# A fused retention and two-layer MLP kernel: three second-layer products of the last chunk's units by a second level of Strassen, with their sums on GpSimd

## The chip, the cores and the metric

The kernel runs on one core of a Trainium2 chip. Its time is device microseconds of one launch; the median of three runs before the change is 630.89 us (630.62 to 631.08). Five engines work from queues of their own, each in order: TensorE (PE, matrix products into PSUM), VectorE (DVE), ScalarE (ACT), GpSimd (POOL) and SyncE (SP, which starts transfers). Everything is computed in f32.

## The reference

A retention layer gives 3072 tokens of 512 features; a two-layer MLP with a leaky ReLU follows. Nearly all arithmetic lies in the MLP.

```python
state = np.zeros((B, H, D, D), dtype=np.float32)
for t in range(S):                                   # B, H, S, D = 4, 8, 768, 64
    state = gamma * state + np.einsum('bhd,bhe->bhde', k[:, :, t], v[:, :, t])
    y[:, :, t] = scale * np.einsum('bhd,bhde->bhe', q[:, :, t], state)
x = y.transpose(0, 2, 1, 3).reshape(B * S, H * D)    # 3072 x 512
h = x @ w_in                                         # 512 x 2048
out = np.maximum(0.01 * h, h) @ w_out                # 2048 x 512
```

## The kernel before

**Tiling.** The sequence is cut into six chunks c = 0 to 5 of 128 steps; with four batches a chunk is 512 tokens, held as 2 x 2 blocks of 256 x 256 (`x`, 128 partitions x 4 blocks x 2 x 256). The 2048 hidden features are four units u = 0 to 3 of 512. A unit of the first layer makes the hidden tile `g` (four blocks), a unit of the second adds g's product with 512 rows of w_out to the chunk's output tile `o` (the result is `os[c]`, four blocks).

**Strassen.** All these 2 x 2 block products are done with seven products M1 to M7 in place of eight, in the form that shares sums (Winograd's). A weight unit holds seven operands (blocks 0 to 3 and three sums); a moving tile holds four blocks and three differences, made by `differences` (L636, four DVE subtractions). Chunks 0 and 1 use one level: seven products of 256 x 256, each of four TensorE products with 256 columns. From chunk 2 on the loop at the end of the kernel goes over n = 0 to 15, with c = 2 + n // 4 and u = n % 4 (`at_of`), and uses two levels:

- The first layer is 7 x 7 = 49 products of 128 x 128, in two groups: `inner(n, 0)` has four of the outer seven (28 products), `inner(n, 1)` three (21). Its steps (L1390) run in the order M1, M5, M4, M6, M2, M3, M7; five results of a step are copied from PSUM by ACT (L1394 to L1402), the others are added by DVE. `outer(n, 0)` and `outer(n, 1)` (L1416) are two and five DVE additions that put the outer level together, and four `leaky` activations of ACT (L1432) follow on outer(n, 1).
- The second layer, for n = 3 to 14, is split. Four of the seven outer products are the *leaves* (`leaf_steps`, L1304): 28 products of 128 x 128 (L1311), in the step order M1, M5, M2, M6, M4, M3, M7. Their moving sums are made by POOL in `leaf_sums` (L1283, four instructions of 128 x 512 over the last blocks of the g tile), their results are kept apart and added to `os[c]` one unit later by `add_results` (L1333, one DVE addition 2048 wide). The other three outer products, operands 0, 4 and 5, are the *trunk* (`trunk`, L1344): 12 products of 256 columns (L1351), which pile up in the PSUM banks 5, 7 and 4 over the units of a chunk. `trunk_taken` (L1356) and its `rest` take them out once, after the chunk's last unit on this path: for chunk 5 in n = 14.
- n = 15, the last unit, has a plain one-level second layer (`output`, whose products are L674), in the order M1, M5, M6, M4, M2, M7, M3, with a store after each block of `os[5]` is complete; M3 goes in three pieces, each with a store of its own.

**Order.** The order is written out by hand; each engine takes its instructions as the loop issues them. In a pass n: add_results (the leaves of n - 1), differences of g(n), inner(n + 1, 0), outer(n + 1, 0), leaf_sums(n), trunk(n), inner(n + 1, 1), outer(n + 1, 1), the leaves of n with the leaky activations of n + 1 set between their copies. In n = 14 the leaky activations stand one by one between the first leaf steps, and differences of g(15) after the fourth.

**Banks.** PSUM has eight banks. inner uses 0 to 3, the leaves 0, 2, 1 and 6, the trunk 5, 7 and 4. In Strassen's steps M1's result is copied to the bank of M6 and M7, M2 is added on M1's bank, M3 on M5's and M7 on M6's, so each later product waits for the copy of the earlier.

The last passes of the loop before the change:

```python
        if leaves:
            moving = leaf_sums(n, behind if not scores_next else None)
            trunk(n, part)
...
        if last_leaves:
            rest = trunk_taken(n, os[c])
            if n + 2 == N2:
                rest()
```

Of the kernel before, what the change touches and what calls it, by code (L numbers as in the profile page):

```python
# [9 lines left out]
FP32 = mybir.dt.float32  # L10
# [6 lines left out]
ALU = mybir.AluOpType  # L17

C = 128
# [3 lines left out]
def kernel(  # L23
# [14 lines left out]
    nc = tc.nc  # L38
    NC = S // C
    DM = H * D  # L40
    HP = H // 2
    NU = DF // 512
    N = B * C // 2
# [4 lines left out]
    work = ctx.enter_context(tc.tile_pool(name="work", bufs=1))  # L48
# [31 lines left out]
    def unit(k):  # L80
        if k not in units:
            units[k] = unit_tile(k, f"w{k}")
        return units[k]
# [11 lines left out]
    step = dec[:, HP * C + NC * H :]  # L95
# [10 lines left out]
    AHEAD = 2  # L106
# [98 lines left out]
    def new_t(c, name):  # L205
        return work.tile([128, 3, 2, N], FP32, tag=f"t{c % 2}", name=name)

    def new_o(c, name="o"):
        return work.tile([128, 4, 2, N], FP32, tag=f"o{int(c > 0)}", name=f"{name}_{c}")
# [408 lines left out]
    def plus(out, a, b):  # L618
        return nc.vector.tensor_tensor(out=out, in0=a, in1=b, op=ALU.add)  # L619
# [186 lines left out]
    def tile_x(c):  # L806
        return work.tile([128, 4, 2, N], FP32, tag="x", bufs=2, name=f"x_{c}")
# [3 lines left out]
        return [x, new_t(c, f"t_{c}")]  # L811

    slot = [0]
    last_four = {}

    class Reversed:

# [6 lines left out]
    def new_g(c, u):  # L824
        i = slot[0]
        slot[0] = 1 - i
        both = work.tile([128, 7, 2, N], FP32, tag=f"g{i}", name=f"g_{c}_{u}")
        last_four[c, u] = both[:, 1:5]
        return u, both[:, 0:4], Reversed(both)

    def run(steps, at):
# [27 lines left out]
    x, t = xs[0]  # L859
# [25 lines left out]
    for s in range(2):  # L885
        part = mask[ts(s, 64), 0 : 3 - s : 2 - s]
# [3 lines left out]
    os = {}  # L890
# [18 lines left out]
    def scratch(name, n):  # L909
# [22 lines left out]
        out=dec[:, 0:n_gq], in_=spread.rearrange("p i n -> p (i n)")))  # L932
# [88 lines left out]
    made = {}  # L1021
# [48 lines left out]
    N2 = (NC - 2) * NU  # L1070

    def at_of(n):
        return 2 + n // NU, n % NU
# [78 lines left out]
    for u in range(NU):  # L1152
        for c in range(2) if u > 0 else ():
# [3 lines left out]
            at = rounds(1, 3)  # L1157
            at = put(at, **hidden_more.get((c, u), {}))
            run(hidden(c, u, *xs[c], *parts[c][1:]), at)
        for c in range(2 if u < NU - 1 else 1):  # L1160
            if u == 0:
                os[c] = new_o(c)
            at = rounds(1, 4 - c) if u < NU - 1 else {}
            at = put(at, **output_more.get((c, u), {}))
# [4 lines left out]
    bank = [ffs.tile([128, 4 * C], FP32, tag="ff", bufs=4, name=f"bank{i}") for i in range(4)]  # L1169
# [25 lines left out]
    def flat_of(part):  # L1195
        return part.rearrange("p i k n -> p (i k n)")
# [106 lines left out]

    def leaf_steps(n, moving):  # L1304

        ps = [bank[i].rearrange("p (i n) -> p i n", i=4) for i in (0, 2, 1, 6)]
        results = leaf_results(n)
        leaf_weights[:] = of_unit.pop(n, leaf_weights)
        for m, q, j, s in LEAVES:
            for i, to in enumerate(TARGETS):  # L1310
                nc.tensor.matmul(ps[q][:, to], lhsT=leaf_weights[i][j], rhs=moving[s][:, i],  # L1311
                                 start=(i == 0 and m in ("M1", "M5", "M4")), stop=True,
                                 skip_group_check=True)
            if m == "M1":
                nc.scalar.copy(out=ps[3], in_=ps[0])
            elif m == "M3":
                plus(results[:, :, 1], results[:, :, 1], ps[1])
            elif m == "M7":
                plus(results[:, :, 3], results[:, :, 3], ps[3])
            else:  # L1320
                nc.scalar.copy(out=results[:, :, {"M5": 3, "M4": 2, "M6": 1, "M2": 0}[m]],
                               in_=ps[q])
            yield

        plus(results[:, :, 2], results[:, :, 2], ps[3])
        plus(results[:, 2], results[:, 2], results[:, 3])
        if at_of(n)[1] > 0:
            unadded.append(lambda: plus(flat_of(os[at_of(n)[0]]), flat_of(os[at_of(n)[0]]),
                                        results.rearrange("p i q n -> p (i q n)")))

    unadded = []

    def add_results():  # L1333

        while unadded:
            unadded.pop()()
# [7 lines left out]
    def trunk(n, part):  # L1344

        u, g, gd = part
        first = n == FIRST_LEAVES or u == 0
        for x, sa, rhs in (("A", 0, g[:, 0]), ("C", 4, gd[:, 0]), ("B", 5, gd[:, 1])):
            for i in range(2):
                for k in range(2):  # L1350
                    nc.tensor.matmul(room[x][:, i, :],  # L1351
                                     lhsT=block(2 * u + 1, sa)[:, k, ts(i, 128)],
                                     rhs=rhs[:, k, :], start=(first and i == 0 and k == 0),
                                     stop=(k == 1), skip_group_check=True)
# [92 lines left out]
    def products(steps, n):  # L1447

        for _ in range(n):
            next(steps, None)  # L1450
# [38 lines left out]
    for n in range(N2):  # L1489
        c, u = at_of(n)  # L1490
        more, visiting, leaves = n + 1 < N2, visits(n), by_leaves(n)
        scores_next = visiting and following(c + 1, 2 * u)
        last_leaves = leaves and (u == NU - 1 or n + 2 == N2)
        if u == 0 and not leaves:
            os[c] = new_o(c)
        if u > 0:
            add_results()
        if more:
            differences(*gs[n][1:])
            if n > 0:  # L1500
                begun = inner_steps(n + 1, 0, held=visiting)
                products(begun, 1)
            while held:
                held.pop()()
            products(begun, 7)
        part = gs.pop(n)
        behind = None
        if visiting:
            if u == 0:
                xs[c + 1] = new_x(c + 1)  # L1510
            joint_visit(c + 1, 2 * u)
            if leaves:
                load_rows(n, range(4)[2 if u == 0 else 0 :])
        elif leaves and u == NU - 1:
            behind = sums_of_x(c + 1, 1)
        if more:
            outer(n + 1, 0)
        if leaves and u == 0:
            finish_chunk(c - 1)
            os[c] = new_o(c)  # L1520
        if visiting and u == 1:
            behind = differences(*xs[c + 1])
        elif c + 1 < NC and u == 2:
            behind = sums_of_x(c + 1, 0)
        if leaves:
            moving = leaf_sums(n, behind if not scores_next else None)
            trunk(n, part)
            if visiting and not scores_next:
                fill(6, 2, start=False)
        else:  # L1530
            steps = output(c, os[c], [part], u == 0, u == NU - 1, room=room if more else last_room,
                           order=FUSED if more else LAST, held=held if more else None)
            products(steps, 3)
        if last_leaves:
            rest = trunk_taken(n, os[c])
            if n + 2 == N2:
                rest()
        if scores_next and leaves:
            scores_of_pair(*scores_next, [bank[i] for i in (1, 6, 2, 3)], second_mask_last=True)
        elif scores_next:  # L1540
            scores_of_pair(*scores_next)
        if visiting:
            load_unit(n + 2, 0)
        if not leaves:
            products(steps, 1)
        if n in (0, 1):
            keep.append(sums_of_rows(n))
        if n in (1, 2):
            keep.append(sums_of_rows(n + 1, nc.gpsimd))
        if more:  # L1550
            inner(n + 1, 1)
            if last_leaves and n + 2 < N2:
                rest()
            for i in range(2) if visiting else ():
                ahead(c + 2, 2 * u + i)
            if keep:
                keep.pop(0)()
            if not leaves:
                products(steps, 1)
            later = [] if leaves else None  # L1560
            outer(n + 1, 1, later)
        if leaves:
            leaf = leaf_steps(n, moving)
            last_one = n + 2 == N2
            for count, ready in ((1, 1), (1, 1), (2, 2)) if last_one else (
                    (4, 2 if u == NU - 1 else 3), (1, 2 if u == NU - 1 else 1)):
                products(leaf, count)
                for _ in range(ready):
                    later.pop(0)()
            if last_one:  # L1570
                differences(*gs[n + 1][1:])
            products(leaf, 8)
            if last_one:
                add_results()
        else:
            products(steps, 3)
        if by_leaves(n + 1) and n + 1 >= NU:
            if not visits(n + 1):
                load_rows(n + 1)
            elif u == NU - 1:  # L1580
                load_rows(n + 1, range(2))
# [92 lines left out]
```

## Time and profile before

| what | value |
|---|---|
| median of three runs | 630.89 us |
| the profiled execution | 631.22 us |
| its span, first to last instruction | 629.3 us |
| TensorE clock granted | full speed throughout |
| n = 12: 546.43 to 568.84 us, DVE busy / ACT / POOL | 17.67 / 10.36 / 5.89 us of 22.41 |
| n = 13: 568.84 to 591.25 us | 15.34 / 10.20 / 5.49 us of 22.41 |
| n = 14: 591.25 to 613.65 us | 21.20 / 11.01 / 5.83 us of 22.40 |
| n = 15 and the last stores: 613.65 to 629.30 us | 10.77 / 0.70 / 0.00 us of 15.65 |

Times in the profile are microseconds from the span's start. A row of a timeline gives the start, the length, the engine, the line, the operation, the tiles written and read, the shape, how many instructions the row merges, and in brackets the idle time before it and what ended that. The busy time of TensorE overlaps from product to product, so the pace is read from the distance between starts. DVE's additions are all on L619 and its subtractions on L622, the lines of the helpers `plus` and `minus`: they are told apart by their tiles. DVE instructions without a dependence start some 0.08 us before the one ahead ends.

### The profile page before, as it was taken

Reading aid. Unit: us, or ns where it says so; the run is one execution under the profiler, and the core shown is the slowest. Engines: PE = TensorE matmul, PEld = TensorE weight load, DVE = VectorE, ACT = ScalarE, POOL = GpSimd, SP = SyncE. Lnnn points to the kernel's source line nnn. Section 1 sums busy time; section 2 is a strip of 40 time slices with the busy share of each in tenths; the row PEclk is TensorE's granted clock in tenths of the full one; section 3 lists DMA queues with packets and bytes.
Section 4 is the critical chain, followed back from the end, with each engine's and each line's share of the span. In section 5 each row is a group of like instructions: output and inputs, shape, how many; then the busy total and the mean of one; then the engine's idle time right before and its main releaser. Section 6 shows DMA issues by size and latency. Waiting matters only on the chain.

```text
span 629.3 us, 15220 instructions
## 1 busy us (share of the span) xinstructions
PE 622.8 (99%) x6375; PEld 572.2 (91%) x6375; DVE 512.4 (81%) x793; ACT 281.4 (45%) x543; POOL 105.8 (17%) x109
## 2 busy tenths in 40 slices
PE   8999999999999999999999999999999999999997
PEld 5888888888888889899999999999999999999996
DVE  5679769889979986679888968789968689977796
ACT  5876646446444114352433433534514435534540
POOL 2000000000010110105133052331250321333030
PEclk9999999999999999999999999999999999999999
DMA  8941425547782998396976996988478568678601
GB/s 328 405 143 34 126 75 193 167 133 252 243 296 73 347 333 272 101 339 190 349 228 215 283 333 240 324 280 280 150 257 298 156 216 281 209 264 278 205 1 68
DMA packets 105939, 140.99 MB, mean 224 GB/s; under 512 B 4488, under 2 KB 84232, under 8 KB 105872
## 3 DMA queue, kind: packets, MB, share of 16 engines
q1 hardware_dynamic: 105568, 139.41, 66.6%
q8 instruction: 50, 0.82, 0.5%
q10 hardware_dynamic: 304, 0.62, 0.3%
q14 instruction: 17, 0.14, 0.1%
HBM read 113.54 MB, written 26.48 MB: 222 GB/s over the span
## 4 chain that ended last, share of the span: by engine, by line
PE 94%; DVE 2%; ACT 1%; DMA 1%; issue 0%; SPq 0%; DVEq 0%; ACTq 0%
PE bank L1390 27%; PE bank L1311 12%; PE bank L1351 10%; PE bank L674 9%; PE C_h L674 4%; PE B_o L674 4%; PE A_h L674 4%; PE A_o L674 4%; PE C_o L674 4%; PE B_h L674 4%; PE D_o L674 2%; PE D_h L674 2%; PE d L695 2%; DMA raw<-in_weights_dram 1%; PE bank L371 1%; PE bank L453 1%
## 5 line engine op out<-in xcount | busy, mean ns | idle before, releaser
L619 DVE TENSOR_TENSOR made<-made,bank 128x512 f32<-128x512 f32 (+1 forms) x96 | 55.9, 617 | 39.8 <-PE bank L1390 35.9
L1390 PEld LDWEIGHTS bank<-x,wb 128*128 128x128 f32 x672 | 77.4, 192 | 1.2 <-ACT bank L1394 0.2
L1390 PE MATMUL bank<-x,wb 128*128 128x128 f32 x672 | 78.4, 276 | 0.0
L622 DVE TENSOR_TENSOR g<-g 128x512 f32<-128x512 f32 x96 | 64.0, 688 | 5.2 <-ACT g L1432 0.5
L1390 PE MATMUL bank<-x,wa 128*128 128x128 f32 x512 | 67.7, 275 | 0.0
L1394 ACT COPY bank<-bank 128x512 f32<-128x512 f32 (+1 forms) x32 | 16.6, 517 | 104.6 <-PE bank L1390 97.4
L1390 PEld LDWEIGHTS bank<-x,wa 128*128 128x128 f32 x512 | 62.7, 192 | 0.5 <-ACT made L1400 0.2
L1390 PE MATMUL bank<-t,wa 128*128 128x128 f32 x384 | 53.4, 275 | 0.0
L619 DVE TENSOR_TENSOR g<-made 128x512 f32<-128x512 f32 x64 | 49.0, 786 | 2.9
L1351 PE MATMUL bank<-g,w 128*128 128x256 f32 x216 | 48.5, 381 | 0.0
L1390 PEld LDWEIGHTS bank<-t,wa 128*128 128x128 f32 x384 | 48.0, 192 | 0.0
L1311 PE MATMUL bank<-g,w 128*128 128x128 f32 x368 | 47.0, 276 | 0.0
L1351 PEld LDWEIGHTS bank<-g,w 128*128 128x128 f32 x216 | 40.3, 190 | 5.4
L1311 PEld LDWEIGHTS bank<-g,w 128*128 128x128 f32 x368 | 43.8, 192 | 0.0
L1432 ACT ACTIVATE g<-g 128x512 f32<-128x512 f32 x64 | 37.7, 633 | 6.9 <-DVE g L619 6.9
L1290 POOL TENSOR_TENSOR x<-g 128x512 f32<-128x512 f32 x12 | 16.6, 1382 | 138.2 <-DVE t L622 40.1
L674 PE MATMUL bank<-g,w 128*128 128x256 f32 x168 | 38.0, 382 | 0.0
L674 PEld LDWEIGHTS bank<-g,w 128*128 128x128 f32 x168 | 31.3, 190 | 4.2
L619 DVE TENSOR_TENSOR o<-o,bank 128x512 f32<-128x512 f32 (+2 forms) x44 | 26.5, 633 | 9.8 <-ACT bank L788 4.2
L619 DVE TENSOR_TENSOR o<-o,w 128x2048 f32<-128x2048 f32 (+2 forms) x17 | 28.9, 1722 | 0.2
L674 PE MATMUL A_h<-x,w 128*128 128x256 f32 x112 | 26.6, 380 | 0.0
L163 POOL TENSOR_TENSOR in<-in,dec 128x512 f32<-128x512 f32 x2 | 2.4, 1232 | 139.7 <-DMA in<-in_kv_dram 139.7
(257 smaller groups left out, 1261.1 us busy)
## 6 DMA issues: line engine op xcount, KB each, us to landing
wa<-kept SPq DMA_DIRECT2D x16, 1344.0 KB, 8.7
w<-leaf_kept SPq DMA_DIRECT2D x44, 448.0 KB, 5.4
raw<-in_weights_dram SPq DMA_DIRECT2D x31, 512.0 KB, 4.4
wb<-kept SPq DMA_DIRECT2D x16, 896.0 KB, 6.0
wa<-kept SPq DMA_DIRECT2D x16, 448.0 KB, 4.7
wb<-kept SPq DMA_DIRECT2D x16, 448.0 KB, 6.8
out_dram<-o SPq DMA_DIRECT2D x23, 256.0 KB, 2.9
kept<-w SPq DMA_DIRECT2D x12, 448.0 KB, 5.7
```

The lines of the kernel that those rows point to most:

```text
L371: nc.tensor.matmul(at[j][ts(h, 64), n, m, i], lhsT=x[ts(j, 64), 1, a, ts(h, 64)], rhs=x[ts(j, 64), 0, a, ts(h, 64)], start=(n == 0 and a = ...
L453: mm = nc.tensor.matmul(at[n][j][ts(i, 64), m, ts(h, 64)], lhsT=val[ts(h, 64), 2 * a + j], rhs=weights[j][ts(h, 64), n, m, i], start=(n == ...
L619: return nc.vector.tensor_tensor(out=out, in0=a, in1=b, op=ALU.add)
L622: return nc.vector.tensor_tensor(out=out, in0=a, in1=b, op=ALU.subtract)
L674: nc.tensor.matmul(to, lhsT=block(w, sa)[:, k, ts(i, 128)], rhs=rhs[:, k, a:z], start=(first and (i == 0 or split) and n == 0 and k == 0), ...
L695: nc.tensor.matmul(banks[r][:, i, :], lhsT=block(2 * u, r + 2 * kh)[:, k, ts(i, 128)], rhs=x[:, 2 * kh + th, k, :], start=(step == 0 and i ...
L1290: op = nc.gpsimd.tensor_tensor(out=out, in0=a, in1=b, op=ALU.subtract)
L1311: nc.tensor.matmul(ps[q][:, to], lhsT=leaf_weights[i][j], rhs=moving[s][:, i], start=(i == 0 and m in ("M1", "M5", "M4")), stop=True, skip ...
L1351: nc.tensor.matmul(room[x][:, i, :], lhsT=block(2 * u + 1, sa)[:, k, ts(i, 128)], rhs=rhs[:, k, :], start=(first and i == 0 and k == 0), s ...
L1390: nc.tensor.matmul(ps[q][:, i], lhsT=w[:, j, i], rhs=part_of(moving[i], s), start=(i == 0 and m in ("M1", "M5", "M4")), stop=True, skip_gr ...
L1394: nc.scalar.copy(out=ps[3], in_=ps[0])
L1432: nc.scalar.activation(g[:, i], g[:, i], AF.Prelu, alpha=0.01)
```

## The change

For n = 12, 13 and 14, the first three units of chunk 5, the trunk's three products also go to the second level: 21 products of 128 x 128 in place of 12 with 256 columns. The leaves' loop becomes `quartered`, used for both. `trunk_weights(n)` makes the four sums of the weights, and `trunk_sums(n)` those of g(n), each with eight POOL instructions (four of 128 x 128 and four of 128 x 256), in tiles that earlier work has given up. `trunk_by_leaves` runs the products in the banks 4, 5, 7 and 6, takes them out in every unit, and adds them in n = 13 and 14 with one 1536-wide DVE addition. At the end of n = 14 POOL combines the three results (`trunk_combined`, four instructions of 128 x 512), and DVE adds the last of them to two blocks of the output in n = 15 (`trunk_all_taken`). trunk_taken and rest are no longer run in n = 14. In chunk 5 add_results moves from the head of a pass to behind outer(n + 1, 0), and the leaves of n = 14 are added in n = 15, after the fourth of its products. The weight sums for n = 12 are issued in n = 9, behind outer's products; those for n = 13 and 14 one pass ahead.

```diff
--- before.py
+++ after.py
@@ -811,7 +811,7 @@
         return [x, new_t(c, f"t_{c}")]
 
     slot = [0]
-    last_four = {}
+    last_four, last_seven = {}, {}
 
     class Reversed:
 
@@ -826,6 +826,7 @@
         slot[0] = 1 - i
         both = work.tile([128, 7, 2, N], FP32, tag=f"g{i}", name=f"g_{c}_{u}")
         last_four[c, u] = both[:, 1:5]
+        last_seven[c, u] = both
         return u, both[:, 0:4], Reversed(both)
 
     def run(steps, at):
@@ -1303,12 +1304,21 @@
 
     def leaf_steps(n, moving):
 
-        ps = [bank[i].rearrange("p (i n) -> p i n", i=4) for i in (0, 2, 1, 6)]
         results = leaf_results(n)
         leaf_weights[:] = of_unit.pop(n, leaf_weights)
+        ps = [bank[i].rearrange("p (i n) -> p i n", i=4) for i in (0, 2, 1, 6)]
+        yield from quartered(ps, leaf_weights, [[x[:, i] for x in moving] for i in range(4)],
+                             results, TARGETS)
+        plus(results[:, 2], results[:, 2], results[:, 3])
+        if at_of(n)[1] > 0:
+            unadded.append(lambda: plus(flat_of(os[at_of(n)[0]]), flat_of(os[at_of(n)[0]]),
+                                        results.rearrange("p i q n -> p (i q n)")))
+
+    def quartered(ps, weights, moving, results, targets):
+
         for m, q, j, s in LEAVES:
-            for i, to in enumerate(TARGETS):
-                nc.tensor.matmul(ps[q][:, to], lhsT=leaf_weights[i][j], rhs=moving[s][:, i],
+            for i, to in enumerate(targets):
+                nc.tensor.matmul(ps[q][:, to], lhsT=weights[i][j], rhs=moving[i][s],
                                  start=(i == 0 and m in ("M1", "M5", "M4")), stop=True,
                                  skip_group_check=True)
             if m == "M1":
@@ -1317,16 +1327,82 @@
                 plus(results[:, :, 1], results[:, :, 1], ps[1])
             elif m == "M7":
                 plus(results[:, :, 3], results[:, :, 3], ps[3])
+                plus(results[:, :, 2], results[:, :, 2], ps[3])
             else:
                 nc.scalar.copy(out=results[:, :, {"M5": 3, "M4": 2, "M6": 1, "M2": 0}[m]],
                                in_=ps[q])
             yield
 
-        plus(results[:, :, 2], results[:, :, 2], ps[3])
-        plus(results[:, 2], results[:, 2], results[:, 3])
+    AT_ENDS = (slice(0, 1), slice(5, 7))
+    end_rooms = {}
+
+    def by_leaves_all(n):
+        return N2 - NU <= n < N2 - 1
+
+    def quarters_of(x):
+        return [x[:, :, k, ts(h, C)] for k in range(2) for h in range(2)]
+
+    def trunk_weights(n):
+
+        if "r" not in end_rooms:
+            end_rooms["r"] = new_o(0, "r")
+        r = flat_of(end_rooms["r"])[:, 0 : 12 * C].rearrange("p (j i n) -> p j i n", j=4, i=3)
+        blocks = unit(2 * at_of(n)[1] + 1)
+        for step in range(4):
+            for to, at in zip((slice(0, 1), slice(1, 3)), AT_ENDS):
+                a11, a21, a12, a22 = quarters_of(blocks[:, at])
+                mine = [r[:, j, to] for j in range(4)]
+                a, b = ((a21, a22), (mine[0], a11), (a12, mine[1]), (a11, a21))[step]
+                nc.gpsimd.tensor_tensor(out=mine[step], in0=a, in1=b,
+                                        op=ALU.subtract if step else ALU.add)
+        trunk_tiles[n] = [[blocks[:, at, 0, 0:C], blocks[:, at, 1, 0:C], blocks[:, at, 1, C:]]
+                          + [r[:, j, i] for j in range(4)] for i, at in enumerate((0, 5, 6))]
+
+    trunk_tiles = {}
+
+    def trunk_sums(n):
+
+        if "sums" not in end_rooms:
+            end_rooms["sums"] = [work.tile([128, 2, HP, C], FP32, tag=tag, bufs=AHEAD,
+                                           name=f"trunk_{tag}") for tag in ("qk", "kv", "kv")]
+        made = [x.rearrange("p s a t -> p (s a) t")[:, 0:3] for x in end_rooms["sums"]]
+        both = last_seven[at_of(n)]
+        for step in range(4):
+            for to, at in zip((slice(0, 1), slice(1, 3)), AT_ENDS):
+                b11, b12, b21, b22 = quarters_of(both[:, at])
+                mine = [x[:, to] for x in made]
+                out, a, b = ((mine[0], b12, b11), (mine[1], b22, mine[0]), (mine[2], b21, mine[1]),
+                             (b12, b22, b12))[step]
+                nc.gpsimd.tensor_tensor(out=out, in0=a, in1=b, op=ALU.subtract)
+        moving = []
+        for i, at in enumerate((0, 5, 6)):
+            b11, b12, b21, b22 = (x[:, 0] for x in quarters_of(both[:, at : at + 1]))
+            moving.append([b11, b21, *(x[:, i] for x in made), b22, b12])
+        return moving
+
+    def trunk_by_leaves(n, moving):
+
+        if "all" not in end_rooms:
+            end_rooms["all"] = new_t(0, "trunk_all")
+            end_rooms["new"] = tile_x("trunk")[:, 0:3]
+        to = end_rooms["all" if at_of(n)[1] == 0 else "new"]
+        ps = [bank[i][:, 0 : 3 * C].rearrange("p (i n) -> p i n", i=3) for i in (4, 5, 7, 6)]
+        products(quartered(ps, trunk_tiles.pop(n), moving, flat_of(to).rearrange(
+            "p (i q n) -> p i q n", i=3, q=4), range(3)), 8)
         if at_of(n)[1] > 0:
-            unadded.append(lambda: plus(flat_of(os[at_of(n)[0]]), flat_of(os[at_of(n)[0]]),
-                                        results.rearrange("p i q n -> p (i q n)")))
+            plus(end_rooms["all"], end_rooms["all"], to)
+
+    def trunk_combined(o):
+
+        a, ab, abc = (end_rooms["all"][:, i] for i in range(3))
+        for out, x, y in ((ab, ab, a), (abc, abc, ab), (o[:, 0], o[:, 0], a),
+                          (o[:, 2], o[:, 2], ab)):
+            nc.gpsimd.tensor_tensor(out=out, in0=x, in1=y, op=ALU.add)
+
+    def trunk_all_taken(o):
+
+        abc = end_rooms["all"][:, 2]
+        plus(o[:, 1:4:2], o[:, 1:4:2], abc.unsqueeze(1).to_broadcast([128, 2, 2, N]))
 
     unadded = []
 
@@ -1490,10 +1566,10 @@
         c, u = at_of(n)
         more, visiting, leaves = n + 1 < N2, visits(n), by_leaves(n)
         scores_next = visiting and following(c + 1, 2 * u)
-        last_leaves = leaves and (u == NU - 1 or n + 2 == N2)
+        last_leaves = leaves and u == NU - 1
         if u == 0 and not leaves:
             os[c] = new_o(c)
-        if u > 0:
+        if u > 0 and c < NC - 1:
             add_results()
         if more:
             differences(*gs[n][1:])
@@ -1505,6 +1581,8 @@
             products(begun, 7)
         part = gs.pop(n)
         behind = None
+        if by_leaves_all(n):
+            trunk_moving = trunk_sums(n)
         if visiting:
             if u == 0:
                 xs[c + 1] = new_x(c + 1)
@@ -1518,23 +1596,28 @@
         if leaves and u == 0:
             finish_chunk(c - 1)
             os[c] = new_o(c)
+        elif more and c == NC - 1:
+            add_results()
         if visiting and u == 1:
             behind = differences(*xs[c + 1])
         elif c + 1 < NC and u == 2:
             behind = sums_of_x(c + 1, 0)
         if leaves:
             moving = leaf_sums(n, behind if not scores_next else None)
-            trunk(n, part)
+            if by_leaves_all(n):
+                trunk_by_leaves(n, trunk_moving)
+            else:
+                trunk(n, part)
             if visiting and not scores_next:
                 fill(6, 2, start=False)
         else:
             steps = output(c, os[c], [part], u == 0, u == NU - 1, room=room if more else last_room,
                            order=FUSED if more else LAST, held=held if more else None)
             products(steps, 3)
+            if not more:
+                trunk_all_taken(os[c])
         if last_leaves:
             rest = trunk_taken(n, os[c])
-            if n + 2 == N2:
-                rest()
         if scores_next and leaves:
             scores_of_pair(*scores_next, [bank[i] for i in (1, 6, 2, 3)], second_mask_last=True)
         elif scores_next:
@@ -1543,14 +1626,20 @@
             load_unit(n + 2, 0)
         if not leaves:
             products(steps, 1)
+            if not more:
+                add_results()
         if n in (0, 1):
             keep.append(sums_of_rows(n))
         if n in (1, 2):
             keep.append(sums_of_rows(n + 1, nc.gpsimd))
         if more:
             inner(n + 1, 1)
-            if last_leaves and n + 2 < N2:
+            if last_leaves:
                 rest()
+            if n == N2 - NU - 3:
+                trunk_weights(N2 - NU)
+            elif by_leaves_all(n) and by_leaves_all(n + 1):
+                trunk_weights(n + 1)
             for i in range(2) if visiting else ():
                 ahead(c + 2, 2 * u + i)
             if keep:
@@ -1571,7 +1660,7 @@
                 differences(*gs[n + 1][1:])
             products(leaf, 8)
             if last_one:
-                add_results()
+                trunk_combined(os[c])
         else:
             products(steps, 3)
         if by_leaves(n + 1) and n + 1 >= NU:
```

## The prediction, made before the changed kernel was run

> **What bounds it now.** I read the busy shares first, then the chain of waits in order of time, then the timelines of VectorE (DVE), GpSimd (POOL) and ScalarE (ACT) over the last four units.
>
> ```profile
> PE 622.8 (99%) x6375; PEld 572.2 (91%) x6375; DVE 512.4 (81%) x793; ACT 281.4 (45%) x543; POOL 105.8 (17%) x109
> ```
>
> ```profile
> 597.50 5.18 PE bank L1351 x24
> 602.68 4.69 PE bank L1390 x42
> 607.37 6.28 PE bank L1311 x56
> 613.65 10.41 PE bank L674 x52
> 624.08 2.04 DVE o L619 x5
> ```
>
> TensorE (PE) sets the time without a gap until its last products; then additions of DVE and the last store end the run. An f32 product leaves two records, so L1351 x24 is the trunk's 12 products of 256 columns (5.18 us, 0.432 each) and L1390 x42 is 21 products of 128 columns (4.69 us, 0.223 each). What the change saves lies in the L1351 row; what it adds lies on ACT, DVE and POOL. DVE and POOL meet, as the timelines of unit 13 show (start, us):
>
> ```profile
> 573.78 1.27 POOL L1290 TENSOR_TENSOR x<-g 128x512 f32<-128x512 f32 x1 [16.18 <-DVE g L622]
> 575.13 1.28 POOL L1290 TENSOR_TENSOR wb<-g,x 128x512 f32<-128x512 f32 x1
> 576.49 1.27 POOL L1290 TENSOR_TENSOR more_room<-g,wb 128x512 f32<-128x512 f32 x1
> 577.72 1.72 POOL L1290 TENSOR_TENSOR g<-g 128x512 f32<-128x512 f32 x1
> ```
>
> ```profile
> 574.31 2.11 DVE L619 TENSOR_TENSOR made<-made,bank 128x512 f32<-128x512 f32 x3 [0.69 <-PE bank L1390]
> 576.52 1.78 DVE L619 TENSOR_TENSOR made<-made 128x512 f32<-128x512 f32 x1
> 578.41 1.57 DVE L619 TENSOR_TENSOR g<-made 128x512 f32<-128x512 f32 x1
> ```
>
> The three DVE additions with a PSUM input run beside POOL at their usual 0.69 us. The two with both inputs in SBUF take 1.78 and 1.57: the first ends 0.54 us after the POOL instruction it met (577.76), and POOL's next, begun at 577.72, takes 1.72 for 1.27, as it waits in turn. They alternate, a pair taking some 1.68 us (0.55 + 1.13). The tail of DVE:
>
> ```profile
> 612.01 2.89 DVE L622 TENSOR_TENSOR g<-g 128x512 f32<-128x512 f32 x4
> 614.83 1.87 DVE L619 TENSOR_TENSOR w<-w,bank 128x512 f32<-128x512 f32 x3
> 616.73 0.69 DVE L619 TENSOR_TENSOR w<-w 128x512 f32<-128x512 f32 x1
> 617.46 2.29 DVE L619 TENSOR_TENSOR o<-o,w 128x2048 f32<-128x2048 f32 x1
> 619.86 2.01 DVE L619 TENSOR_TENSOR o<-o,bank 128x256 f32<-128x256 f32 x5
> 622.36 0.69 DVE L619 TENSOR_TENSOR o<-o,bank 128x512 f32<-128x512 f32 x1 [0.49 <-PE bank L674]
> 624.08 2.04 DVE L619 TENSOR_TENSOR o<-o,bank 128x512 f32<-128x512 f32 x5 [1.04 <-PE bank L674]
> ```
>
> Ahead of these lie the five instructions of outer(15, 1), 608.87 to 612.09. From there on DVE idles for 1.5 us in all (0.49 and 1.04), and POOL does nothing: its last instruction ended at 604.86.
>
> **What the Trainium skill says.** "SBUF — State Buffer", section "Who interferes with whom": a DVE instruction with two SBUF inputs contends with a GpSimd instruction that reads SBUF, one holding the pair for its whole instruction while the other is blocked; with at most one SBUF input it doesn't contend. The trace agrees (0.69 against 1.57 and 1.78). "GPSIMD Engine Reference", section "3.1 Elementwise — side-by-side cycle accounting": about 2.6 cycles per element for two inputs, at 1.2 GHz by my estimate 1.11 us for 512 elements; the trace has 1.27, so some 0.16 is paid per instruction. For 128 and 256 elements I take POOL's rows of another stage, the least disturbed ones:
>
> ```profile
> 311.50 0.46 POOL L1249 TENSOR_TENSOR w<-last 128x128 f32<-128x128 f32 x1 [13.28 <-DMA leaf_kept<-w]
> 312.84 0.73 POOL L1249 TENSOR_TENSOR w<-last 128x256 f32<-128x256 f32 x1 [0.88 <-DMA leaf_kept<-w]
> ```
>
> **The change part by part.**
>
> (1) Products. In n = 12, 13 and 14 the trunk goes from 5.18 to 4.69 us: 0.49 saved each. But its third step, M2, overwrites the bank that M1's copy reads, and with three products to a step it is due 1.34 us after the start (6 x 0.223). M1 is over at 0.67; ACT starts 0.20 later (the 384-wide copy at 536.16, its products over at 535.96), takes 0.48, and PE goes on 0.15 after that (in the leaves, where a copy ended at 541.65, M2 from 541.77 on ran 0.03 late). So 1.50 against 1.34: 0.16 lost. Net 0.33 a unit, 1.0 for three.
>
> (2) trunk_sums, on POOL ahead of leaf_sums: 4 x (0.46 + 0.73) = 4.8 us a unit. It needs only leaky(0) and the first two differences, so POOL begins 1.4 us into the differences. In n = 13 that is 572.2, less the 0.3 gained before; with three or four waits of 0.3 to 0.5 on DVE it ends near 578.2. The M7 products that need the last sum are due at 575.1 - 0.3 + 4.2 + 0.2 = 579.2: 1 us of cover, nothing charged. In n = 12 and 14 the 2.2 us addition of the leaves' results (in n = 14 moved from ahead of the differences to behind outer) stands in DVE's queue just about then; I have it behind the last sum. If it goes ahead, PE waits for what is left after the cover, some 1 to 2 us.
>
> (3) trunk_weights, 4.8 us on POOL after leaf_sums, due a unit later: hidden behind a whole unit. It meets outer's five and delays them some 2.5 us; the differences then end 0.5 to 1 us later than now, and 6.25 us of inner products lie between them and the trunk. The first set, in n = 9, does the same near 496 to 501. Taken as nothing; 0 to 0.5 is kept for the range.
>
> (4) Evictions. Five ACT copies, 2.4 us a unit, on an engine that is 45% busy. Three 384-wide DVE additions (1.5) and in n = 13 and 14 a 1536-wide one (between 1.22 for 1024 and 2.29 for 2048: 1.75). Gone in n = 14: trunk_taken and rest, 3 x 0.6 + 0.69 + 1.22 = 3.7. DVE is busy 15.3 to 21.2 of 22.4 us in these units, so PE isn't held by this alone.
>
> (5) The end, where the time is lost. PE is 1.0 early at leaf(14): 606.4. POOL's order in n = 14 is trunk_sums, over at about 600.4; leaf_sums, 5.3 and the two long additions that get in between (2.2 and 1.6), over at 608.9; then trunk_combined, 4 x 1.27, at once. outer(15, 1), five DVE instructions with two SBUF inputs, starts at 607.9. Each has to let one of POOL's last five pass: 5 x 1.65 = 8.2, so it ends at 616.1 and not at 612.1. ACT's leaky instructions wait for it, and behind them in ACT's queue stand the leaves' copies: M6's comes at 612.9 and holds the M7 products 1.3 us; M4's at 617.3 holds M5 of the last unit, in the same bank, 1.8 us. PE ends at 606.4 + 6.2 (leaves) + 1.3 + 1.8 + 12.2 (52 records: 10.41, and the last step 1.76) = 627.9, against 625.8.
>
> DVE is later still. From 616.1 it has no gap: four differences 2.75, the leaves' additions 1.8 and 0.7, M5's pieces 0.75, M6 0.65, the new trunk_all_taken 1.15 (1024 wide), M4 0.65, the addition of the leaves' results 2.25, M2 0.6, M7 1.2, M3's pieces 0.8: 13.3 in all, less 0.15 of overlaps. It ends at 629.25, against 626.13: +3.1. The four stores come within 2 us, 1 MB at up to 372 GB/s (the DMA view's highest here), 2.8 us; begun near 627.4, they are through about when the last piece would land anyway. 0 to 0.5; zero taken.
>
> Sum: span 629.3 + 3.1 = 632.4; the profiled execution, 631.22, becomes 634.3. The median of the runs shown is 0.33 below it: 634.0.
>
> **Rivals.** A, the forecast: with POOL's instructions 10% shorter or longer the same steps end 1 sooner or 2 later, so 632.5 to 636.5.
>
> B: POOL is late inside the trunk too. One 2.2 us addition, or two alternations of 1.68, get ahead of the last sums, and PE waits 0.7 to 2.5 us in two or three units. For it: only 1 us of cover in (2), and POOL's demand goes from 5.5 to over 15 of a unit's 22 us, while DVE's instructions with two SBUF inputs ask 10 to 13 of the same 22. Against: the sums begin before the differences are over. About 4 on top: 638.
>
> C, not slower: POOL is through leaf_sums and trunk_combined before outer(15, 1) begins. The point is 607.9: if POOL is done there, outer takes its 3.2, the 1.5 us of idle DVE take in trunk_all_taken, and PE ends the run 1.0 sooner: 629.9. For it: the additions that trunk_combined waits for are over by 606.6. Against: 4.8 + 5.3 + 5.3 = 15.4 us of POOL from 594.7 on, with no wait at all, end at 610.1. It needs shorter instructions or milder contention than the rows shown; halfway is 631 to 632.
>
> That 21 weight loads in place of 12 eat the saving is a fourth; the row at 602.68 speaks against it, with just these loads at 0.223 a product.
>
> **Numbers.** A 0.58, B 0.20, C 0.22. A difference under 0.2% (1.3 us) can't be told from none. C falls about evenly to faster and same, and a little of A to same: faster 0.10, same 0.13, slower 0.77. The range, 630.2 to 638.0, leaves out half of C and the upper half of B.
>
> **What would show it.** Right: trunks of about 4.85 us; leaf(14) 1.0 earlier; outer(15, 1) over 7 us long beside trunk_combined; waits of PE on ACT in leaf(14) and in the last unit; DVE without idle over its last 13 us and done over 1 us after PE. Wrong: gaps of PE on POOL inside a trunk (B), outer(15, 1) near 3.2 us (C), or a last store landing much more than 3.2 us after DVE.

## The result

| | median | runs |
|---|---|---|
| before | 630.79 us | 630.42 to 632.56 (6) |
| changed | 635.69 us | 634.98 to 637.55 (6) |

The ratio is 1.008, with a 95% interval of 1.0061 to 1.0098: slower by 4.9 us, where 3.2 on this median were forecast (634.0). The changed kernel's profiled execution, 637.55 us, is its longest. It is already 1.85 us behind the execution before at the start of trunk(12), from stages that the change leaves alone, so times below are compared from that start on: 552.52 us before, 554.37 after. From there to the end of the span the kernel before takes 76.8 us and the changed one 81.3, 4.5 more.

The trunks, from the chain of waits in order of time of the changed kernel (start, length, engine, tile and line; L1321 are now the products of leaves and trunk, L1466 those of inner):

```profile
554.53 4.84 PE bank L1321 x42
...
577.34 4.84 PE bank L1321 x42
```

They take 4.84 us, as forecast, instead of 5.18. The end, first PE in leaf(14), which starts at 608.77, from its M4 on:

```profile
612.38 1.06 PE L1321 MATMUL bank<-more_room,w 128*128 128x128 f32 x8
614.38 1.16 PE L1321 MATMUL bank<-g,w 128*128 128x128 f32 x8 [0.94 <-ACT w L1332]
616.57 1.13 PE L1321 MATMUL bank<-g,w 128*128 128x128 f32 x8 [1.03 <-ACT w L1332]
617.54 1.89 PE L674 MATMUL bank<-g,last 128*128 128x256 f32 x8
619.95 8.93 PE L674 MATMUL bank<-g,last 128*128 128x256 f32 x44 [0.52 <-ACT w L1332]
```

PE waits three times for ACT: for the copies of M5 and M6 within the leaves and for that of M4 ahead of the last unit's M5. ACT in turn:

```profile
613.22 0.63 ACT L1508 ACTIVATE g<-g 128x512 f32<-128x512 f32 x1 [2.79 <-DVE g L619]
613.76 0.57 ACT L1332 COPY w<-bank 128x512 f32<-128x512 f32 x1
614.83 0.63 ACT L1508 ACTIVATE g<-g 128x512 f32<-128x512 f32 x1 [0.51 <-DVE g L619]
615.37 1.05 ACT L1332 COPY w<-bank 128x512 f32<-128x512 f32 x2
618.19 1.23 ACT L1508 ACTIVATE g<-g 128x512 f32<-128x512 f32 x2 [1.76 <-DVE g L619]
```

Each copy (L1332) stands behind a leaky activation (L1508), and that waits for DVE. DVE and POOL at that time:

```profile
607.54 2.67 DVE L619 TENSOR_TENSOR trunk_all<-trunk_all,x_trunk 128x1536 f32<-128x1536 f32 x1
610.13 1.47 DVE L619 TENSOR_TENSOR made<-made,bank 128x384 f32<-128x384 f32 x3
611.71 1.42 DVE L619 TENSOR_TENSOR g<-made 128x512 f32<-128x512 f32 x1
613.05 1.75 DVE L619 TENSOR_TENSOR g<-g,made 128x512 f32<-128x512 f32 x1
614.72 1.76 DVE L619 TENSOR_TENSOR made<-made 128x512 f32<-128x512 f32 x1
616.51 2.24 DVE L619 TENSOR_TENSOR g<-made 128x512 f32<-128x512 f32 x2
```

```profile
607.33 1.27 POOL L1291 TENSOR_TENSOR more_room<-g,wb 128x512 f32<-128x512 f32 x1
608.56 2.79 POOL L1291 TENSOR_TENSOR g<-g 128x512 f32<-128x512 f32 x1
611.31 2.94 POOL L1400 TENSOR_TENSOR trunk_all<-trunk_all 128x512 f32<-128x512 f32 x2
614.21 3.39 POOL L1400 TENSOR_TENSOR o<-o,trunk_all 128x512 f32<-128x512 f32 x2
```

outer(15, 1), the last four DVE rows, runs from 611.71 to 618.75: 7.0 us for what took 3.2 before:

```profile
608.87 0.69 DVE L619 TENSOR_TENSOR g<-made 128x512 f32<-128x512 f32 x1
609.48 0.68 DVE L619 TENSOR_TENSOR g<-g,made 128x512 f32<-128x512 f32 x1
610.08 0.69 DVE L619 TENSOR_TENSOR made<-made 128x512 f32<-128x512 f32 x1
610.80 1.29 DVE L619 TENSOR_TENSOR g<-made 128x512 f32<-128x512 f32 x2
```

In the changed kernel its first four instructions each let one of trunk_combined's four (L1400) pass; only the fifth is free. The three additions at 610.13, which read PSUM, keep their 0.55 us beside POOL. What follows on DVE has hardly a gap:

```profile
623.99 1.41 DVE L619 TENSOR_TENSOR o<-o,bank 128x256 f32<-128x256 f32 x4
625.50 1.23 DVE L619 TENSOR_TENSOR o<-o,trunk_all 128x1024 f32<-128x1024 f32 x1
626.64 0.68 DVE L619 TENSOR_TENSOR o<-o,bank 128x512 f32<-128x512 f32 x1
627.35 2.29 DVE L619 TENSOR_TENSOR o<-o,w 128x2048 f32<-128x2048 f32 x1
629.75 2.61 DVE L619 TENSOR_TENSOR o<-o,bank 128x512 f32<-128x512 f32 x6
```

PE ends at 630.63, DVE at 632.36: 1.7 us after it, against 0.3 before.

### The profile page after: what moved, and what is told of

It is laid out like the page before. It is cut to its first block, busy times and chain, and to the rows that moved or that the text cites. A ratio compares the mean times of both kernels' runs of the same rounds, so it can differ in the third digit from the quotient of the medians.

```text
span 635.7 us, 15428 instructions
## 1 busy us (share of the span) xinstructions
PE 624.2 (98%) x6429; PEld 573.5 (90%) x6429; DVE 529.0 (83%) x800; ACT 288.1 (45%) x557; POOL 155.3 (24%) x161
## 4 chain that ended last, share of the span: by engine, by line
PE 85%; DVE 6%; DMA 5%; ACT 2%; issue 1%; SPq 0%; DVEq 0%; ACTq 0%
PE bank L1466 23%; PE bank L674 9%; PE bank L1321 9%; PE bank L1427 7%; PE C_h L674 4%; PE B_o L674 4%; PE A_h L674 4%; PE C_o L674 4%; PE A_o L674 4%; PE B_h L674 4%; DMA wa<-kept 3%; PE D_o L674 2%; PE D_h L674 2%; DVE g L619 2%; PE d L695 2%; DVE made L619 2%
## 5 line engine op out<-in xcount | busy, mean ns | idle before, releaser
L1466 PE MATMUL bank<-x,wb 128*128 128x128 f32 x672 | 78.3, 276 | 0.0
L1466 PEld LDWEIGHTS bank<-x,wb 128*128 128x128 f32 x672 | 77.1, 192 | 1.0
L622 DVE TENSOR_TENSOR g<-g 128x512 f32<-128x512 f32 x96 | 66.5, 713 | 4.8 <-ACT g L1508 0.5
L1466 PE MATMUL bank<-x,wa 128*128 128x128 f32 x512 | 67.8, 275 | 0.0
L1466 PEld LDWEIGHTS bank<-x,wa 128*128 128x128 f32 x512 | 62.7, 192 | 0.6 <-ACT made L1476 0.2
L619 DVE TENSOR_TENSOR g<-made 128x512 f32<-128x512 f32 x64 | 52.9, 847 | 2.9
L1321 PE MATMUL bank<-g,w 128*128 128x128 f32 x404 | 52.9, 277 | 2.1 <-ACT w L1332 2.0
L1466 PE MATMUL bank<-t,wa 128*128 128x128 f32 x384 | 53.5, 276 | 0.4 <-DMA wa<-kept 0.3
L1321 PEld LDWEIGHTS bank<-g,w 128*128 128x128 f32 x404 | 48.4, 192 | 3.0 <-issue 1.2
L1466 PEld LDWEIGHTS bank<-t,wa 128*128 128x128 f32 x384 | 48.0, 192 | 0.8 <-DMA wa<-kept 0.8
L1508 ACT ACTIVATE g<-g 128x512 f32<-128x512 f32 x64 | 37.9, 634 | 11.5 <-DVE g L619 11.5
L1291 POOL TENSOR_TENSOR x<-g 128x512 f32<-128x512 f32 x12 | 17.9, 1495 | 85.5 <-PE bank L1466 33.8
L674 PE MATMUL bank<-g,w 128*128 128x256 f32 x168 | 38.0, 382 | 0.0
L674 PEld LDWEIGHTS bank<-g,w 128*128 128x128 f32 x168 | 31.3, 190 | 4.2
L417 POOL MEMSET between<- 128x1 f32 x16 | 1.9, 118 | 132.9 <-PE bank L453 104.9
L1427 PE MATMUL bank<-g,w 128*128 128x256 f32 x144 | 32.5, 382 | 0.0
L1427 PEld LDWEIGHTS bank<-g,w 128*128 128x128 f32 x144 | 26.9, 190 | 3.7
```

Source lines behind the costliest of these rows:

```text
L417: done = nc.gpsimd.memset(between, 0.0).ins
L674: nc.tensor.matmul(to, lhsT=block(w, sa)[:, k, ts(i, 128)], rhs=rhs[:, k, a:z], start=(first and (i == 0 or split) and n == 0 and k == 0), ...
L1291: op = nc.gpsimd.tensor_tensor(out=out, in0=a, in1=b, op=ALU.subtract)
L1321: nc.tensor.matmul(ps[q][:, to], lhsT=weights[i][j], rhs=moving[i][s], start=(i == 0 and m in ("M1", "M5", "M4")), stop=True, skip_group_c ...
L1427: nc.tensor.matmul(room[x][:, i, :], lhsT=block(2 * u + 1, sa)[:, k, ts(i, 128)], rhs=rhs[:, k, :], start=(first and i == 0 and k == 0), s ...
L1466: nc.tensor.matmul(ps[q][:, i], lhsT=w[:, j, i], rhs=part_of(moving[i], s), start=(i == 0 and m in ("M1", "M5", "M4")), stop=True, skip_gr ...
```

## The experiments

Each was timed in five rounds beside the kernel before, on one chip for each set of four (before: 631.06 us in the first set, 630.68 in the second). "PE end" and "DVE end" are counted from the start of trunk(12) in the profiled execution, where the kernel before has 73.3 and 73.6 us, the changed one 76.3 and 78.0.

| run | median us | ratio to before (95%) | outer(15, 1) us | PE end | DVE end |
|---|---|---|---|---|---|
| e1_comb_dve | 634.00 | 1.0046 (1.0034 to 1.0058) | 3.2 | 73.9 | 76.4 |
| e2_comb_late | 632.63 | 1.0032 (1.0020 to 1.0044) | 3.2 | 73.5 | 75.0 |
| e3_no_comb | 631.95 | 1.0018 (1.0011 to 1.0025) | 3.2 | 74.3 | 74.8 |
| e4_add_first | 635.58 | 1.0072 (1.0060 to 1.0084) | 7.7 | 76.9 | 77.4 |
| e5_products | 630.78 | 1.0000 (0.9992 to 1.0008) | 3.2 | 72.9 | 73.4 |
| e6_ballast | 635.94 | 1.0081 (1.0067 to 1.0095) | 7.2 | 78.0 | 78.3 |
| e7_memsets | 630.61 | 1.0002 (0.9994 to 1.0010) | 3.2 | 73.3 | 73.6 |
| e8_all_late | 632.93 | 1.0036 (1.0023 to 1.0048) | 3.2 | 72.8 | 75.7 |

The theory is the forecast's: POOL and DVE take turns on instructions that read SBUF, trunk_combined meets outer(15, 1), and DVE, ACT and PE are late one behind the other. Its rivals: DVE simply has too much to do at the end; or the loss lies in the trunks.

**e1_comb_dve.** The four additions on another engine, at the same place:

```diff
-            nc.gpsimd.tensor_tensor(out=out, in0=x, in1=y, op=ALU.add)
+            nc.vector.tensor_tensor(out=out, in0=x, in1=y, op=ALU.add)
```

> The four additions of trunk_combined go from POOL to DVE, at the same place in the program. Theory (exclusive meeting of POOL and DVE in outer(15,1)): outer(15,1) meets only the last of leaf_sums and takes about 4 us instead of 7.0, the waits of PE on ACT in leaf(14) (2.3 us in the changed kernel) and in the last unit (0.7) shrink to under 0.5 together; DVE gets 2.5 us more to do at its end, so about 1 us faster than the changed kernel, 634 to 635. Rival (DVE is simply given too much work at the end, contention or not): the 2.5 us of additions come on top, 637 to 638.

634.0: the theory's range. DVE got four more instructions and yet ended 1.6 us sooner, because outer(15, 1) fell back to 3.2 us and PE's waits on ACT from three to two, 0.4 and 0.6 us. That is more than the theory left: leaf(14) still takes 7.4 us, 1.1 more than before.

**e2_comb_late.** The same instructions on POOL, behind the last difference of g(15):

```diff
-                differences(*gs[n + 1][1:])
+                behind = differences(*gs[n + 1][1:])
...
+            if behind is not None:
+                tc.add_manual_dep(op.ins, behind.ins.name, IN_ORDER, reason="one port for both")
+                behind = None
```

> trunk_combined stays on POOL but its first instruction waits for the last difference of g(15), so that outer(15,1) is past. Theory: outer(15,1) about 4 us, hardly a wait of PE on ACT in leaf(14); the addition of M4 then waits for trunk_combined near 2 us, DVE ends about 2 us sooner than in the changed kernel: 633 to 634. Rival (too much work for DVE): no change, 635.5 to 636, as DVE's work is the same.

632.6, rather better than the theory had it. No instruction was taken away, and by the medians 3.1 of the 4.9 us are gone. Not all of that is the place of the four instructions. In the traces DVE ends 3.0 us sooner, counted from trunk(12), but 0.7 of them lie in n = 12, in a wait for a store that the changed kernel's trace has and this one has not (below). From the start of leaf(14) to DVE's end it is 21.4 us against 23.6: 2.2 us were the place. PE still waits 1.2 us in leaf(14), where hardly a wait was expected. The four instructions now meet later ones, two of which take 0.7 us longer each (the addition alone takes 0.69, trunk_all_taken 1.23):

```profile
616.43 1.41 DVE L619 TENSOR_TENSOR w<-w 128x512 f32<-128x512 f32 x1
617.77 1.46 DVE L619 TENSOR_TENSOR o<-o,bank 128x256 f32<-128x256 f32 x4
619.33 1.96 DVE L619 TENSOR_TENSOR o<-o,trunk_all 128x1024 f32<-128x1024 f32 x1
```

**e3_no_comb.** Both trunk_combined and trunk_all_taken left out.

```diff
-            if not more:
-                trunk_all_taken(os[c])
...
-            if last_one:
-                trunk_combined(os[c])
```

> Leaves out trunk_combined and trunk_all_taken, so the trunk's results of chunk 5 are made but not added to the output. Theory: without the four POOL instructions outer(15,1) takes about 4 us, PE runs through leaf(14) and the last unit, and the end is PE's again: 4 us less than the changed kernel, 631 to 632, of which 1.2 is the work of trunk_all_taken itself. Rival (too much work): only trunk_all_taken's 1.2 us is gone, 634.5. Second rival (the loss lies in the trunks of n = 12 to 14 or in their evictions): 634.5 to 635.5 too, with the gaps of PE where they were.

631.95: the theory again, 3.7 us less than the changed kernel. 0.9 us over before remain. Its trace shows why: PE loses 1.1 us in leaf(14), by waits of 0.4 and 0.6 us on ACT, because outer(15, 1) still starts 2.9 us after the leaves do (1.7 before), and 0.9 us in and behind leaf(12) by the wait for a store, below. Together that is 2.0 us against the 1.0 that the products save.

**e4_add_first.** The addition of the leaves back at the head of a pass in chunk 5. With that in n = 14 comes the one in n = 15, which again stands ahead of all additions of the last unit's products, as in the kernel before.

```diff
-        if u > 0 and c < NC - 1:
+        if u > 0:
             add_results()
...
-        elif more and c == NC - 1:
-            add_results()
```

> In chunk 5 the addition of the leaves goes back to the head of a pass (for n = 14; n = 13 has none), ahead of the differences. Theory: it runs without POOL beside it (2.3 us instead of 3.35), but the differences and trunk_sums of n = 14 come 2.2 us later, and PE waits about 0.7 us for the last sums within trunk(14); leaf_sums end about where they did, so outer(15,1) still meets trunk_combined: 635.5 to 637. Rival (the moved addition, stretched to 3.35 us in the way of POOL, is what makes POOL late at the end): outer(15,1) is free, 632 to 633.

635.58, no better: the moved addition isn't what makes POOL late. The waits of PE on POOL that the move avoids came as worked out, here in trunk(14) of this kernel:

```profile
599.27 0.71 PE L1321 MATMUL bank<-trunk_kv,r 128*128 128x128 f32 x4 [0.28 <-POOL trunk_kv L1376]
599.82 0.39 PE L1321 MATMUL bank<-trunk_kv,w 128*128 128x128 f32 x2
600.38 0.71 PE L1321 MATMUL bank<-trunk_kv,w 128*128 128x128 f32 x4 [0.17 <-POOL trunk_kv L1376]
```

Counted from start to start they cost 0.45, 0.33 and, at M7, 0.1 us; with what follows each, trunk(14) takes 6.0 us, 1.2 more than in the changed kernel.

**e5_products.** Besides what e3 leaves out, the sums of n = 13 and 14 and the 1536-wide additions are gone; the products read the sums of n = 12.

```diff
-                nc.gpsimd.tensor_tensor(out=out, in0=a, in1=b, op=ALU.subtract)
+                if n == N2 - NU:
+                    nc.gpsimd.tensor_tensor(out=out, in0=a, in1=b, op=ALU.subtract)
...
-        if at_of(n)[1] > 0:
-            plus(end_rooms["all"], end_rooms["all"], to)
```

> Leaves out trunk_combined, trunk_all_taken, the 1536-wide additions, and for n = 13 and 14 trunk_sums and trunk_weights (the products read the sums of n = 12), so only the second-level products and their evictions are left of the change. Theory: the products give what was worked out, 0.33 us a unit, and with POOL no busier than before nothing is lost at the end: 1.0 less than before, 629.8 to 630.2, or up to 0.8 more than that where the leaves' first copy of n = 12 waits for the stores. Rival (the products or their evictions cost what they save): 630.8 to 631.5.

630.78, no gain. The 629.8 to 630.2 of the theory failed; what it allowed for a wait on the stores covers the number, and the rival's range begins right above it. The trace decides between them: the products did save their 1.0 us. leaf(14) starts 54.3 us after trunk(12), 0.4 sooner than before, with 0.6 us of waits in leaf(12) and the inner products behind it on the way. leaf(14) itself runs without a wait, and PE's end is 0.4 us sooner. DVE hands 0.2 of that back, and the last stores the rest:

```profile
619.28 0.69 DVE L619 TENSOR_TENSOR o<-o,bank 128x512 f32<-128x512 f32 x1 [0.97 <-PE bank L674]
620.00 2.29 DVE L619 TENSOR_TENSOR o<-o,w 128x2048 f32<-128x2048 f32 x1
622.40 2.61 DVE L619 TENSOR_TENSOR o<-o,bank 128x512 f32<-128x512 f32 x6
```

The 2048-wide addition now stands behind M4's, after DVE's idle time and not in it. Even with its sums for nothing, the change would have brought too little to measure, as long as the wait in n = 12 stays.

**e6_ballast and e7_memsets.** The kernel before, with instructions on POOL that nobody needs, behind leaf_sums of n = 14: seven additions, or fourteen memsets of the same width.

```diff
+            if n + 2 == N2:
+                room_of = new_t(0, "ballast")[:, 0]
+                for _ in range(7):
+                    nc.gpsimd.tensor_tensor(out=room_of, in0=unit(1)[:, 0], in1=unit(1)[:, 5],
+                                            op=ALU.add)
```

```diff
+            if n + 2 == N2:
+                room_of = new_t(0, "ballast")[:, 0]
+                for _ in range(14):
+                    nc.gpsimd.memset(room_of, 0.0)
```

> The kernel before, plus seven POOL additions of 128 x 512 behind leaf_sums of n = 14, which read weights and write a tile that nobody reads. No work is added on PE, DVE or ACT. Theory (POOL and DVE take turns on instructions that read SBUF): outer(15,1) takes 7 to 8 us instead of 3.2, PE waits on ACT in leaf(14) and in the last unit as in the changed kernel, and the end comes 2.5 to 4 us later: 633.3 to 635. Rival (the changed kernel's loss is its added DVE work and waits, not the meeting): no change, 630.8 to 631.2.

> The kernel before, plus fourteen POOL memsets of 128 x 512 at the same place: POOL is busy, but reads nothing. Theory (what counts is that POOL reads SBUF): outer(15,1) keeps its 3.2 us, 630.8 to 631.2. Rival (any POOL instruction in the way is enough): outer(15,1) is drawn out and the time goes up by 1 us or more.

The additions cost 5.3 us, as much as the whole change and more than the 2.5 to 4 that were expected (4.7 of it in the trace up to DVE's end); the memsets cost nothing. POOL and then DVE in e6_ballast:

```profile
604.75 11.55 POOL L1530 TENSOR_TENSOR ballast<-w 128x512 f32<-128x512 f32 x7
```

```profile
606.51 2.29 DVE L619 TENSOR_TENSOR o<-o,w 128x1024 f32<-128x1024 f32 x1
608.72 1.47 DVE L619 TENSOR_TENSOR made<-made,bank 128x384 f32<-128x384 f32 x3
610.29 1.53 DVE L619 TENSOR_TENSOR g<-made 128x512 f32<-128x512 f32 x1
611.75 1.75 DVE L619 TENSOR_TENSOR g<-g,made 128x512 f32<-128x512 f32 x1
613.42 1.76 DVE L619 TENSOR_TENSOR made<-made 128x512 f32<-128x512 f32 x1
```

and in e7_memsets:

```profile
604.22 8.10 POOL L1530 MEMSET ballast<- 128x512 f32 x14
```

```profile
608.29 0.69 DVE L619 TENSOR_TENSOR g<-made 128x512 f32<-128x512 f32 x1
608.90 0.68 DVE L619 TENSOR_TENSOR g<-g,made 128x512 f32<-128x512 f32 x1
609.50 0.69 DVE L619 TENSOR_TENSOR made<-made 128x512 f32<-128x512 f32 x1
```

The same three instructions of outer(15, 1) take 1.5 to 1.8 us beside POOL's additions and 0.69 beside its memsets. So it is POOL's reading that counts, and it alone is enough for the loss: e6 adds no work to PE, DVE or ACT, and its PE shows the waits of the changed kernel at the same three places, and one more of 1.0 us, on DVE, among the last unit's last products.

**e8_all_late.** An attempt at a better version: e2, and the 1536-wide addition of n = 14 behind the differences too, o[2] ahead of o[0], and a load of weights moved away from the stores of chunk 4.

```diff
-                behind = differences(*gs[n + 1][1:])
+                differences(*gs[n + 1][1:])
+                behind = unsummed.pop()()
...
-            inner(n + 1, 1)
+            inner(n + 1, 1, held=n == N2 - NU)
...
+            if n == N2 - NU:
+                load_unit(n + 2, 1)
```

> As e2_comb_late, and besides: the 1536-wide addition of n = 14 goes behind the differences of g(15), o[2] is combined before o[0], and the weights that are loaded beside the stores of chunk 4 (second group, n = 12) are asked for only after the leaves. Theory: outer(15,1) starts about 1.2 us sooner, the 1.0 us wait of PE in leaf(14) and the wait for the stores in n = 12 are gone, and DVE ends about 1 us sooner than in e2_comb_late: 631.0 to 632.0. Rival (DVE's amount of work sets the end whatever the order): 632.3 to 632.9.

632.93, as e2: the theory's 631.0 to 632.0 failed, and here the rival is right. The waits in leaf(14) are gone and PE ends at 72.8, 0.4 sooner than before, but DVE ends at 75.7: from the start of leaf(14) it takes 21.5 us, as in e2. What is taken out ahead of outer(15, 1) comes back behind it, on an engine that has no idle time left. The wait in leaf(12) also stayed (0.4 us in it and 0.2 behind). That doesn't clear the load: it moved in the program, but SyncE's queue sent it 2.3 us after the first store, as in the changed kernel.

## Why the forecast was right, and what it mis-sized

The sign, the mechanism and its place were right: outer(15, 1) against trunk_combined, ACT's copies behind the leaky activations, PE on ACT, DVE last. The size was 1.7 us short on the median, 1.4 of it within the profile from trunk(12) on (4.5 against 3.1), and two of its terms were wrong by over 1 us and cancelled, which is luck. Step by step:

- (1) Products: forecast 0.33 us a unit. Right: 4.84 us a trunk, so 0.34. M2 waits for M1's copy in each.
- (2) trunk_sums: no wait, right in all three units, with the order of the additions as assumed. e4 shows how near it was: 2.3 us of addition put ahead cost PE 1.2 us.
- (3) trunk_weights: nothing, right; that of n = 9 shows no gap of PE in or behind it.
- A wait that the forecast doesn't have, in n = 12. ACT's first copy of the leaves writes the tile that the stores of chunk 4 still read, and waits for them:

```profile
568.06 1.56 ACT L1332 COPY o<-bank 128x512 f32<-128x512 f32 x3 [2.50 <-DMA out_dram<-o]
```

  It costs 0.56 us in leaf(12) and 0.18 in the inner products behind it: 0.74 of the 1.0 us saved. leaf(14) started 0.3 us sooner than before, not 1.0.
- (5) outer(15, 1). The start was mis-sized: 2.9 us after leaf(14)'s first product, where the forecast kept the 1.7 of before (its 606.4 is the time of the chain, which counts leaf(14) from 0.16 us later), as the two long additions (2048 and 1536 wide, 3.35 and 2.67 us) both ran alternately with leaf_sums. The number of meetings was four and not five, the last of leaf_sums having met the 1536-wide addition: 7.0 us, not 8.2. So it ended 10.0 us after the start of leaf(14), forecast 9.9: the start came 1.3 us later than forecast and the stretch was 1.2 us shorter. (The end of leaf_sums in the forecast, 608.9, is also not the sum of its terms, which is 609.5.)
- (5) PE's waits: 2.5 us in leaf(14) and 0.7 in the last unit, forecast 1.3 and 1.8. The sum, 3.2 against 3.1, held, though neither term did.
- (5) DVE from there on: 13.6 us, forecast 13.15. The stores: 3.3 us behind DVE, forecast 3.15.

So the terms that make up the missing 1.4 us are the wait of n = 12, counted as nothing (0.7), DVE's own time (0.45), the stores (0.2) and the end of outer(15, 1) (0.1). What e3 and e5 add: with trunk_combined and trunk_all_taken out of the way the change stands at +0.9 us, and with its sums for n = 13 and 14 and the 1536-wide additions left out as well at none. So the 629.9 of rival C was not reached even there; 0.6 us of the distance is the wait in n = 12.

## What to carry over

Before work goes to an idle GpSimd, count how many VectorE instructions with two SBUF inputs are due beside it: each meeting cost VectorE 0.7 to 1.1 us here (1.42 to 1.76 us for what takes 0.69), and what waits behind those instructions pays. Four such instructions cost some 2.2 us more at one place in this kernel than a few us later, where they still lengthened VectorE's work by 1.4: move them before giving them up, and ask first which engine has slack at the end. A saving of 1 us on TensorE was worth nothing here: 0.6 of it went into a wait for a store, and the rest into the additions and stores that finish the run.

## What was not expected of the hardware

**POOL that only writes doesn't hold DVE back.** Fourteen memsets, 0.53 us each, left every DVE instruction beside them at its length. The Trainium skill, "SBUF — State Buffer", section "Who interferes with whom", says so (a GpSimd instruction that only writes doesn't contend with a VectorE instruction that has two SBUF inputs); here both cases stand side by side, 630.6 against 635.9 us.

**An instruction fetch and a load beside a store.** The wait in n = 12 comes and goes among kernels whose code up to there is the same (the changed kernel, e1 to e4). In all traces with the changed code one transfer of 16 KB of the instruction queue lies near the end of the four stores of chunk 4 (packet records, us from the span's start; for the last store packet its end):

```
kernel          first store   fetch, 16 KB        last store packet   ACT's copy
before             559.81     568.30 to 569.44         563.66           564.38
e2_comb_late       559.12     563.72 to 564.64         563.71           564.33
e4_add_first       559.52     564.05 to 564.98         564.05           564.66
after              561.57     565.90 to 566.83         567.04           568.06
e1_comb_dve        558.72     562.89 to 563.81         564.24           565.03
e3_no_comb         558.96     563.39 to 564.31         564.53           565.55
e5_products        558.77     563.01 to 563.93         564.36           565.15
e8_all_late        559.54     563.74 to 564.67         565.10           565.88
```

Where the fetch comes just behind the last packet of the stores, ACT's copy follows 5.1 to 5.2 us after the first store's issue and PE isn't held; where it comes ahead of that packet, 6.3 to 6.6, and of the stores' 512 packets only the last one or two are so late. The Trainium skill, "Runtime: NRT & Kernel Launch", section "Instruction fetch mechanics", says that instructions come in blocks of 16 KiB through a DMA queue of the engine's own; the size agrees. That the fetch is the cause is read from these traces, not shown: a kernel that does nothing but shift the fetch wasn't tried. Nor is it all. In e2 and e4, where the fetch comes late enough, the stores still end 4.5 to 4.6 us after the first issue, against 3.85 before. There a load of weights is the candidate: with the changed code it is sent 2.3 us after the first store, before 2.55, and its first packets start 0.8 us or more ahead of the stores' last in all seven traces, before just behind it.
